# Attention, mixture of experts and feed-forward on one core: another order of the feed-forward's second products, and x loaded in two halves

## The chip, the core and the metric

The kernel runs on one NeuronCore of a Trainium2 chip. The metric is the device time of one execution in microseconds (us). TensorE multiplies into PSUM, VectorE (DVE), ScalarE (ACT) and GpSimd (POOL) do the rest of the arithmetic, and SyncE (SP) issues nearly all DMAs. Each engine works through its own instructions in the order in which they are written.

## The reference, cut to what matters

```python
attn = softmax(mask(q k^T / 8 + bias)) @ v        # 4 x 8 heads, 576 x 64, window 128
x = attn as (2304, 512)
P = exp(x @ w_gate - max); 8 rounds of row and column scaling
out = sum over e of P[:, e] * (relu(x @ w1[e]) @ w2[e])   # 8 experts, 512 -> 1024 -> 512
h = out @ w_in                                    # 512 -> 2048
g = where(h >= 1, h, where(h <= -1, 0, (h + 1)**2 / 4))
return g @ w_out                                  # 2048 -> 512
```

The change concerns the last three lines, the feed-forward, and the loads of x into SBUF.

## The kernel before, in words

Every fp32 operand is split into a high part h (rounded, by ScalarE, line 705 in the feed-forward) and a low part l (the rest, by VectorE, line 708), and one product is three matmuls: high by high (L76), high by low (L77), low by high (L78). This is `mm3`, and one call of it is called a step here.

The feed-forward is cut into three thirds of 768 tokens; a third has eight units of 256 columns of h, taken in pairs. Both its matrix products are done with seven block products in place of eight. For a pair, `g1` runs twice (the first product of unit one, then of unit two, 42 matmuls of 384 columns each, PSUM banks a to d), and then `g2s` once, the second product for both units: 42 steps of three matmuls of 256 columns. It has 21 results (3 blocks n of 128 tokens by 7 block products s); two results share a PSUM bank of tag "g2", of which there are four (bufs=4). So there are eleven fills of a bank, the last with one result. A result needs one step of unit one and one of unit two. When a bank's results are complete, `drain` adds it to `acf` in SBUF (VectorE, L841; in the first pair of a third ScalarE copies it, L839). The fifth fill can start when the first bank is drained.

Before the change, `g2s` begins with unit one's step for the first half of four banks, and then goes bank by bank: unit two's step for the first half, both units' steps for the second half, drain, and unit one's step for the first half of the bank after the next three.

Between the two products stands `put7`, a generator. It makes from the first product of a unit the seven blocks of g and their high and low parts: `choose` (L702) is the piecewise function, whose square ScalarE makes before (L698, L699); blocks 0, 1, 2 are c22, f11, c12; blocks 3, 4 are s13 and 5, 6 are s24, two sums each, made by GpSimd (L726, L727, L731, L732). `hi(n, m)` and `lo(n, m)` make the parts of blocks n to m-1. A unit's `put7` starts in its own `g1` and goes one part further at each tick. A tick comes after each block product of `g1` and after each third step of `g2s`; this sets where its instructions stand on VectorE, ScalarE and GpSimd, between the drains. In a pair, unit one's last part `lo(5, 7)` falls into the last tick before `g2s`, and unit two's `put7` is half done when `g2s` starts. s13 and s24 lie in two buffers of tag "raw", which the next unit's s13 and s24 take over.

`xload` loads the next third's x, high and low, four DMAs each, one every four ticks. In the feed-forward it starts at a third's last `g2s`; the loads then fall into that `g2s` and the first products after it. There too SyncE loads w2 for the first pair of a third, twice over (`w2_prep` is appended by both the previous pair and the first), and writes the third's results to `out` (`combine`, L798).

```python
NPUT = 4
def tick(first): ...      # advances every put7 by one part, then weight loads, x loads, sums
run(g1(i + 1, pools, ps2), True)
run(g2s(i, acc, ps2), False)
```

Of the kernel before, what the change touches and what calls it, by code (L numbers as in the profile page):

```python
# [11 lines left out]
F32 = mybir.dt.float32  # L12
# [17 lines left out]
def attn_moe_ffn(ctx: ExitStack, tc, q, k, v, w_gate, w1, w2, w_in, w_out, out):  # L30
    nc = tc.nc
# [43 lines left out]
    def mm3(ps, lh, ll, rh, rl, first, last, on=False):  # L75
        nc.tensor.matmul(ps, lhsT=lh, rhs=rh, start=first, stop=False, skip_group_check=on)  # L76
        nc.tensor.matmul(ps, lhsT=lh, rhs=rl, start=False, stop=False, skip_group_check=on)  # L77
        nc.tensor.matmul(ps, lhsT=ll, rhs=rh, start=False, stop=last, skip_group_check=on)  # L78
# [323 lines left out]
                    nc.sync.dma_start(out=d[:, :, a - p * TP:z - p * TP], in_=x.bitcast(F32))  # L402

    def xload(p):
        for x, d in zip(xop[p % 2], xd[p]):
            for kk in range(KD):
                nc.sync.dma_start(out=x[:, kk].bitcast(F32), in_=d[:, kk])
                for _ in range(4):
                    yield

    def logits(t0, n, lp, wgs, tag):
        nt = n // P
# [250 lines left out]
    def g1(i, pools, psp):  # L663
        kind, t, e, j = units[i]
        wh, wl = W1.pop(i)
        V, G = nc.vector, nc.gpsimd
        p = phase(i)

        def prod(ps, b, a, first):
            ah, al = (S["h"][:, a], S["l"][:, a]) if isinstance(a, int) else (xq(p, *a), xq(p, *a, True))  # L670
            for kk in range(KH):
                mm3(ps, wh[:, kk, b, :], wl[:, kk, b, :], ah[:, kk, :], al[:, kk, :],
                    first and kk == 0, kk == KH - 1, not first)

        def bank(x):
            return psp.tile([P, TH], F32, tag=x, name=f"ps{x}")

        def tmp(x):
            return tmpp.tile([P, TH], F32, tag=x, name=x)

        def put(c, f, r):

            h, l = (x[:, f, r, :] for x in ht)
            nc.scalar.activation(h, c, AF.Relu)  # L684
            yield "V"
            V.scalar_tensor_tensor(l, c, 0.0, h.bitcast(F32), ALU.max, ALU.subtract)  # L686
            yield ""

        def put7(c11, pc, pd, u2, c22):

            h, l = ht
            hf = h.bitcast(F32)
            f11, c21, c12 = (tmp(x) for x in ("f11", "c21", "c12"))
            g = tp.tile([P, 2, TH], F32, tag="T", name="g")
            s13, s24 = (rawp.tile([P, 2, TH], F32, tag="raw", name=x) for x in ("s13", "s24"))

            def square(c, n):
                nc.scalar.activation(g[:, n], c, AF.Relu, bias=half, scale=0.5)  # L698
                nc.scalar.activation(g[:, n], g[:, n], AF.Square)  # L699

            def choose(o, c, n):
                V.scalar_tensor_tensor(o, c, 1.0, g[:, n], ALU.max, ALU.min)  # L702

            def hi(n, m, x):
                nc.scalar.activation(h[:, n:m], x, AF.Copy)  # L705

            def lo(n, m, x):
                V.tensor_tensor(l[:, n:m], x, hf[:, n:m], ALU.subtract)  # L708

            square(c22, 0)  # L710
            square(c11, 1)
            yield ""
            choose(c22, c22, 0)
            V.tensor_tensor(c21, pc, u2, ALU.add)
            hi(0, 1, c22.unsqueeze(1))
            yield ""
            choose(f11, c11, 1)
            lo(0, 1, c22.unsqueeze(1))
            V.tensor_tensor(c12, pd, u2, ALU.add)
            square(c21, 0)  # L720
            hi(1, 2, f11.unsqueeze(1))
            yield ""
            choose(c21, c21, 0)
            lo(1, 2, f11.unsqueeze(1))
            square(c12, 1)
            G.tensor_tensor(s13[:, 0], c21, c22, ALU.add)  # L726
            G.tensor_tensor(s13[:, 1], f11, c21, ALU.subtract)  # L727
            yield ""
            choose(c12, c12, 1)
            hi(2, 3, c12.unsqueeze(1))  # L730
            G.tensor_tensor(s24[:, 0], s13[:, 0], f11, ALU.subtract)  # L731
            G.tensor_tensor(s24[:, 1], c12, s24[:, 0], ALU.subtract)  # L732
            yield "free"
            lo(2, 3, c12.unsqueeze(1))
            yield "free"
            hi(3, 5, s13)
            yield "free"
            lo(3, 5, s13)
            yield "free"
            hi(5, 7, s24)  # L740
            yield "free"
            lo(5, 7, s24)
            yield "free"

        pa, pb = (bank("a"), bank("b")) if i % 2 == 0 else (bank("b"), bank("a"))
        pc, pd = bank("c"), bank("d")
        p1, u2, u3 = (tmp(x) for x in ("p1", "u2", "u3"))
        prod(pa, 0, (0, 0), True)
        nc.scalar.activation(p1, pa, AF.Copy)  # L749
        yield  # L750
        hop = pools["hop"]
        if kind == 0:
            ht = HT[i] = [hop.tile([P, 2, 2, TH], F32R, tag=f"h{x}", bufs=2, name=f"h{x}") for x in "hl"]
            c12, c21, c22 = (pools["c"].tile([P, TH], F32, tag=x, bufs=2, name=x) for x in ("c12", "c21", "c22"))
        else:
            ht = HT[i] = [hop.tile([P, 7, TH], F32R, tag=f"h{x}", bufs=2, name=f"h{x}") for x in "hl"]
            c22 = tmp("c22")
        prod(pb, 4, 1, True)
        V.tensor_tensor(u2, pb, p1, ALU.add)  # L759
        yield  # L760
        prod(pc, 5, (1, 0), True)
        V.tensor_tensor(u3, pc, u2, ALU.add)  # L762
        yield
        prod(pd, 3, 0, True)
        V.tensor_tensor(c22, pd, u3, ALU.add)  # L765
        yield
        prod(pa, 1, (0, 1), False)
        if kind == 0:
            c11 = put(pa, 0, 0)
            puts.append(c11)  # L770
        else:
            puts.append(put7(pa, pc, pd, u2, c22))
        yield
        prod(pc, 6, (1, 1), False)
        if kind == 0:
            NEXT[c11] = next(c11)
            V.tensor_tensor(c21, pc, u2, ALU.add)  # L777
            puts.append(put(c22, 1, 1))
        yield
        prod(pd, 2, 2, False)  # L780
        if kind == 0:
            V.tensor_tensor(c12, pd, u2, ALU.add)
            puts.append(put(c21, 0, 1))
        yield
        if kind == 0:
            puts.append(put(c12, 1, 0))
# [21 lines left out]
    def g2s(i, acc, psp):  # L808
# [4 lines left out]
        end = i + 2 == NU  # L813
        flat = acc.rearrange("p n s d -> p (n s) d")
        if end:
            order = [(0, 0), (0, 1), (1, 0), (1, 1), (0, 2), (1, 2), (2, 0), (2, 1), (0, 3), (0, 4), (1, 3), (1, 4),
                     (0, 5), (0, 6), (1, 5), (1, 6), (2, 3), (2, 5), (2, 2), (2, 4), (2, 6)]
        else:
            order = [(n, s) for s in range(7) for n in range(NB)]
        banks = [sorted(order[x:x + 2]) for x in range(0, len(order), 2)]  # L820
# [3 lines left out]
        def part(b, x, u):  # L824
            if x == 0 and u == 0:
                PS[b] = psp.tile([P, 2, FU], F32, tag="g2", bufs=4, name="psg2")
            n, s = banks[b][x]
            hh, hl, wh, wl = ops[u]
            ts = slice(n * P, (n + 1) * P)
            mm3(PS[b][:, x], hh[:, s, ts], hl[:, s, ts], wh[:, BLOCK[s]], wl[:, BLOCK[s]], u == 0, u == 1)  # L830
            count[0] += 1
            return count[0] % 3 == 0

        def drain(b):
            f = [n * 7 + s for n, s in banks[b]]
            a = flat[:, f[0]:f[-1] + 1:max(f[-1] - f[0], 1)]
            ps = PS.pop(b)[:, 0:len(f)]
            if first:
                nc.scalar.activation(a, ps, AF.Copy)  # L839
            else:  # L840
                nc.vector.tensor_tensor(a, ps, a, ALU.add)  # L841
# [8 lines left out]
            r0 = t * TP + r * TH + (NB - 1) * P  # L850
            nc.sync.dma_start(out=out[r0:r0 + P, x * FU:(x + 1) * FU], in_=n2[s])

        for b in range(4):
            if part(b, 0, 0):
                yield
        for b in range(len(banks)):
            if b >= 4 and part(b, 0, 0):
                yield
            for x, u in [(0, 1), (1, 0), (1, 1)][:1 if len(banks[b]) == 1 else 3]:
                if part(b, x, u):  # L860
                    yield
            drain(b)
            if end:
                if b in (6, 7):
                    post.append(combine(t, [b - 6], acc, (V, G)))
                elif b == 8:
                    add(V, 5, 1)
                    add(V, 3, 5)
                    add(G, 6, 3)
                elif b == 9:  # L870
                    add(G, 0, 4)
                    add(G, 0, 5)
                    store(0, 1, 0)
                elif b == 10:
                    store(6, 0, 1)
                    add(V, 3, 4)
                    store(3, 1, 1)
                    add(V, 2, 1)
                    store(2, 0, 0)
# [374 lines left out]
```

## Time and profile before

| | |
|---|---|
| median of three runs | 2112.09 us (2112.01 to 2113.35) |
| profiled execution | 2110.97 us, its span 2109.2 us |
| TensorE busy | 2042.0 us (97%), 11719 matmuls |
| VectorE / ScalarE / GpSimd busy | 1336.0 / 746.1 / 728.3 us |
| mean granted TensorE clock | 0.995 |

The span is from the first to the last instruction; the feed-forward takes the part from about 1686 us to the end. TensorE is busy for nearly all of it, but matmuls overlap, so a gap of TensorE shorter than a matmul's latency is not seen as idle: the start times of the matmuls tell more than the idle times.

### The profile page before, as it was taken

How to read it: one execution, taken by the hardware profiler on the slowest of the kernel's cores; microseconds unless marked ns; L12 is line 12 of the kernel's file. 1: busy time of each engine (PE TensorE's matmuls, PEld its weight loads, DVE VectorE, ACT ScalarE, POOL GpSimd, SP SyncE). 2: the span in 40 equal slices, each digit the busy share in tenths (PEclk: the TensorE clock that was granted, in tenths of full speed). 3: DMA queues.
4: the chain of work that ended last, by engine and by line, in shares of the span. 5: the costliest groups of instructions: out<-in, count | busy, mean ns of one | idle time of the engine just before them, and what ended most of it. 6: DMA issues, size and time to landing. Idle time of an engine off the chain costs nothing.

```text
span 2109.2 us, 32062 instructions
## 1 busy us (share of the span) xinstructions
PE 2042.0 (97%) x11719; PEld 1854.7 (88%) x11719; DVE 1336.0 (63%) x2967; ACT 746.1 (35%) x1716; POOL 728.3 (35%) x755
## 2 busy tenths in 40 slices
PE   7999999999999999999999999999999999899997
PEld 5888888998999898998899898999899898898887
DVE  6766655554554756666666666666666667857686
ACT  6777343333333331221121231121121263545452
POOL 4333347666756401112121011111110036645433
PEclk9999999999999999999999999999999999999999
DMA  7333578777777787676677597676676684866762
GB/s 154 86 82 95 205 244 308 244 261 249 255 254 248 270 328 252 245 245 239 234 257 242 208 338 266 234 262 223 233 276 214 215 327 177 315 256 261 281 238 100
DMA packets 238797, 496.91 MB, mean 236 GB/s; under 512 B 70704, under 2 KB 152624, under 8 KB 238640
## 3 DMA queue, kind: packets, MB, share of 16 engines
q1 hardware_dynamic: 222640, 475.34, 63.8%
q10 hardware_dynamic: 16000, 19.53, 3.0%
q8 instruction: 92, 1.51, 0.3%
q14 instruction: 65, 0.53, 0.1%
HBM read 353.39 MB, written 141.03 MB: 234 GB/s over the span
## 4 chain that ended last, share of the span: by engine, by line
PE 82%; DVE 7%; ACT 6%; DMA 3%; issue 1%; SPq 1%; POOL 0%; ACTq 0%; POOLq 0%; DVEq 0%
PE psg L78 15%; PE psg L76 14%; PE psg L77 14%; PE psc L76 3%; PE psc L77 3%; PE psc L78 3%; PE psd L76 3%; PE psd L77 3%; PE psd L78 3%; PE psb L76 2%; PE psb L78 2%; PE psb L77 2%; PE psa L77 2%; PE psa L78 2%; PE psa L76 2%; ACT g L698 2%
## 5 line engine op out<-in xcount | busy, mean ns | idle before, releaser
L78 PE MATMUL psg<-w2h,hl 128*128 128x512 f32 (+1 forms) x1584 | 568.6, 359 | 22.1 <-DVE hl L708 21.5
L76 PE MATMUL psg<-w2h,hh 128*128 128x512 f32 (+1 forms) x1584 | 567.1, 358 | 7.7 <-DVE acc L907 2.7
L77 PE MATMUL psg<-w2l,hh 128*128 128x512 f32 (+1 forms) x1584 | 564.4, 356 | 6.1 <-DMA w2l<-wd2l 6.1
L78 PEld LDWEIGHTS psg<-w2h,hl 128*128 128x128 f32 x1584 | 300.1, 189 | 72.9 <-DVE hl L708 30.5
L907 DVE SCALAR_TENSOR_TENSOR acc<-psg,pt,acc 128x512 f32<-128x512 f32 x252 | 188.2, 749 | 252.1 <-PE psg L78 250.7
L76 PEld LDWEIGHTS psg<-w2h,hh 128*128 128x128 f32 x1584 | 300.3, 190 | 52.1 <-ACT hh L705 8.2
L77 PEld LDWEIGHTS psg<-w2l,hh 128*128 128x128 f32 x1584 | 300.3, 190 | 47.3 <-DMA w2l<-wd2l 7.3
L684 ACT ACTIVATE hh<-c 128x384 fp32r<-128x384 f32 x270 | 140.8, 521 | 87.4 <-DVE c L777 53.8
L686 DVE SCALAR_TENSOR_TENSOR hl<-c,hh 128x384 fp32r<-128x384 f32 x270 | 165.0, 644 | 0.0
L749 ACT ACTIVATE p<-psa 128x384 f32<-128x384 f32 x57 | 28.0, 492 | 368.5 <-PE psa L78 338.6
L76 PE MATMUL psd<-sh,w1h 128*128 128x384 f32 x456 | 153.9, 338 | 1.6 <-DVE c L765 1.6
L78 PE MATMUL psd<-sh,w1l 128*128 128x384 f32 x456 | 153.3, 336 | 0.0
L77 PE MATMUL psd<-sl,w1h 128*128 128x384 f32 x456 | 153.2, 336 | 0.0
L192 POOL TENSOR_TENSOR t<-e 128x128 f32<-128x128 f32 x32 | 15.1, 471 | 372.9 <-DVE e L168 372.9
L193 POOL TENSOR_TENSOR t<-e,t 128x128 f32<-128x128 f32 x32 | 15.5, 484 | 326.7 <-DVE e L168 326.7
L726 POOL TENSOR_TENSOR s<-c,c 128x384 f32<-128x384 f32 x24 | 30.2, 1259 | 283.6 <-DVE c L702 283.6
L82 POOL TENSOR_TENSOR w2l<-raw,w2h 128x512 fp32r<-128x512 f32 x60 | 81.5, 1381 | 117.9 <-ACT w2h L81 117.9
L343 POOL TENSOR_TENSOR s<-s,mx 128x512 f32<-128x512 f32 (+2 forms) x80 | 66.6, 848 | 124.9 <-DVE mx L341 71.5
L759 DVE TENSOR_TENSOR u<-psb,p 128x384 f32<-128x384 f32 x57 | 31.8, 557 | 103.2 <-PE psb L78 79.8
L76 PE MATMUL psc<-x0h,w1h 128*128 128x384 f32 x272 | 92.7, 341 | 1.6 <-DVE u L762 1.6
L78 PE MATMUL psc<-x0h,w1l 128*128 128x384 f32 x272 | 92.4, 340 | 0.0
L77 PE MATMUL psc<-x0l,w1h 128*128 128x384 f32 x272 | 92.3, 339 | 0.0
(273 smaller groups left out, 4725.3 us busy)
## 6 DMA issues: line engine op xcount, KB each, us to landing
w1h<-wd1h SPq DMA_DIRECT2D x84, 896.0 KB, 5.0
w1l<-wd1l SPq DMA_DIRECT2D x84, 896.0 KB, 7.8
raw<-in_moe_w SPq DMA_DIRECT2D x60, 512.0 KB, 4.5
w2h<-wd2h SPq DMA_DIRECT2D x60, 512.0 KB, 5.6
w2l<-wd2l SPq DMA_DIRECT2D x60, 512.0 KB, 6.4
wd1h<-w1h SPq DMA_DIRECT2D x30, 896.0 KB, 6.2
wd1l<-w1l SPq DMA_DIRECT2D x30, 896.0 KB, 6.5
w2h<-wd2h SPq DMA_DIRECT2D x28, 896.0 KB, 8.1
```

Source lines behind the costliest of these rows:

```text
L76: nc.tensor.matmul(ps, lhsT=lh, rhs=rh, start=first, stop=False, skip_group_check=on)
L77: nc.tensor.matmul(ps, lhsT=lh, rhs=rl, start=False, stop=False, skip_group_check=on)
L78: nc.tensor.matmul(ps, lhsT=ll, rhs=rh, start=False, stop=last, skip_group_check=on)
L82: eng.tensor_tensor(l, x, h.bitcast(F32), ALU.subtract)
L343: nc.gpsimd.tensor_tensor(s[:, 0:nj, :nk], s[:, 0:nj, :nk], mx[:, 6:6 + nj].unsqueeze(2).to_broadcast([P, nj, nk]), ALU.mult)
L684: nc.scalar.activation(h, c, AF.Relu)
L686: V.scalar_tensor_tensor(l, c, 0.0, h.bitcast(F32), ALU.max, ALU.subtract)
L698: nc.scalar.activation(g[:, n], c, AF.Relu, bias=half, scale=0.5)
L726: G.tensor_tensor(s13[:, 0], c21, c22, ALU.add)
L749: nc.scalar.activation(p1, pa, AF.Copy)
L759: V.tensor_tensor(u2, pb, p1, ALU.add)
L907: nc.vector.scalar_tensor_tensor(a, ps, sc, a, ALU.mult, ALU.add)
```

## The change

Three edits. In `g2s`, unit one's steps for both halves of four banks come first; then, bank by bank, unit two's two steps, the drain, and, from the second bank on, unit one's two steps for the bank that stands three further on. Only a bank's first step has the start flag, since both halves are now begun before either is complete. For the last pair of all, the results of token block 2 move behind those of blocks 0 and 1. In `put7`, unit one's `hi(5, 7)` and `lo(5, 7)` come three ticks later. In `xload`, the four high parts come three ticks apart, then there is a pause of 20 ticks, and then the four low parts follow, three ticks apart.

```diff
     def xload(p):
-        for x, d in zip(xop[p % 2], xd[p]):
-            for kk in range(KD):
-                nc.sync.dma_start(out=x[:, kk].bitcast(F32), in_=d[:, kk])
-                for _ in range(4):
-                    yield
+        for n in range(2 * KD):
+            lo, kk = divmod(n, KD)
+            nc.sync.dma_start(out=xop[p % 2][lo][:, kk].bitcast(F32), in_=xd[p][lo][:, kk])
+            for _ in range(20 if n == KD - 1 else 3):
+                yield
@@ put7
             lo(3, 5, s13)
             yield "free"
+            for _ in range(3 if i % 2 == 0 else 0):
+                yield "free"
             hi(5, 7, s24)
             yield "free"
             lo(5, 7, s24)
@@ g2s
-            mm3(PS[b][:, x], hh[:, s, ts], hl[:, s, ts], wh[:, BLOCK[s]], wl[:, BLOCK[s]], u == 0, u == 1)
+            mm3(PS[b][:, x], hh[:, s, ts], hl[:, s, ts], wh[:, BLOCK[s]], wl[:, BLOCK[s]], u == 0 and x == 0, u == 1,
+                True)
...
-        for b in range(4):
-            if part(b, 0, 0):
-                yield
-        for b in range(len(banks)):
-            if b >= 4 and part(b, 0, 0):
-                yield
-            for x, u in [(0, 1), (1, 0), (1, 1)][:1 if len(banks[b]) == 1 else 3]:
+        def bank(b, u):
+            for x in range(len(banks[b])):
                 if part(b, x, u):
                     yield
+
+        for b in range(4):
+            yield from bank(b, 0)
+        for b in range(len(banks)):
+            yield from bank(b, 1)
             drain(b)
+            if 1 <= b < len(banks) - 3:
+                yield from bank(b + 3, 0)
             if end:
-                if b in (6, 7):
-                    post.append(combine(t, [b - 6], acc, (V, G)))
+                if b in (5, 6):
+                    post.append(combine(t, [b - 5], acc, (V, G)))
```

What this does to the order of the instructions is shown at three places; they stand in each pair alike (the first two) or once in each of two thirds (the third).

TensorE, the second pair of the first third, where the fifth fill of a bank begins. Unit one's operands are w2h_17434 and hh_17438, unit two's w2h_17448 and hh_17523; psg2 with its number is a fill. Before, the 16th step (of the fourth fill, 17615) and the 17th, which begins the fifth fill (17678):

```order
L76 MATMUL psg2_17615<-w2h_17448,hh_17523 128x256
L77 MATMUL psg2_17615<-w2l_17449,hh_17523 128x256
L78 MATMUL psg2_17615<-w2h_17448,hl_17524 128x256
L76 MATMUL psg2_17678<-w2h_17434,hh_17438 128x256
L77 MATMUL psg2_17678<-w2l_17435,hh_17438 128x256
L78 MATMUL psg2_17678<-w2h_17434,hl_17439 128x256
```

In the changed kernel, the 12th step (of the second fill, 17598) and the 13th, which begins the fifth fill (17662):

```order
L76 MATMUL psg2_17598<-w2h_17448,hh_17523 128x256
L77 MATMUL psg2_17598<-w2l_17449,hh_17523 128x256
L78 MATMUL psg2_17598<-w2h_17448,hl_17524 128x256
L76 MATMUL psg2_17662<-w2h_17434,hh_17438 128x256
L77 MATMUL psg2_17662<-w2l_17435,hh_17438 128x256
L78 MATMUL psg2_17662<-w2h_17434,hl_17439 128x256
```

The fifth fill, which takes the first fill's bank, begins after 12 steps instead of 16, and one bank, two steps, after the first fill's last step instead of three banks and nine steps after it.

VectorE, the same pair, from unit two's first `choose` to the second row after `lo` of c12. hl_17439 is unit one's low part, hl_17524 unit two's; acf is a drain. Before:

```order
L702 SCALAR_TENSOR_TENSOR c22_17525<-c22_17525,g_17563 128x384
L714 TENSOR_TENSOR c21_17561<-psc_17505,u2_17508 128x384
L708 TENSOR_TENSOR hl_17439<-s24_17477,hh_17438 128x768
L702 SCALAR_TENSOR_TENSOR f11_17560<-psb_17503,g_17563 128x384
L708 TENSOR_TENSOR hl_17524<-c22_17525,hh_17523 128x384
L719 TENSOR_TENSOR c12_17562<-psd_17506,u2_17508 128x384
L702 SCALAR_TENSOR_TENSOR c21_17561<-c21_17561,g_17563 128x384
L708 TENSOR_TENSOR hl_17524<-f11_17560,hh_17523 128x384
L702 SCALAR_TENSOR_TENSOR c12_17562<-c12_17562,g_17563 128x384
L841 TENSOR_TENSOR acf_17084<-psg2_17593,acf_17084 128x2x256
L708 TENSOR_TENSOR hl_17524<-c12_17562,hh_17523 128x384
L841 TENSOR_TENSOR acf_17084<-psg2_17597,acf_17084 128x2x256
```

In the changed kernel:

```order
L702 SCALAR_TENSOR_TENSOR c22_17525<-c22_17525,g_17563 128x384
L714 TENSOR_TENSOR c21_17561<-psc_17505,u2_17508 128x384
L702 SCALAR_TENSOR_TENSOR f11_17560<-psb_17503,g_17563 128x384
L708 TENSOR_TENSOR hl_17524<-c22_17525,hh_17523 128x384
L719 TENSOR_TENSOR c12_17562<-psd_17506,u2_17508 128x384
L702 SCALAR_TENSOR_TENSOR c21_17561<-c21_17561,g_17563 128x384
L708 TENSOR_TENSOR hl_17524<-f11_17560,hh_17523 128x384
L702 SCALAR_TENSOR_TENSOR c12_17562<-c12_17562,g_17563 128x384
L708 TENSOR_TENSOR hl_17439<-s24_17477,hh_17438 128x768
L708 TENSOR_TENSOR hl_17524<-c12_17562,hh_17523 128x384
L844 TENSOR_TENSOR acf_17085<-psg2_17591,acf_17085 128x2x256
L844 TENSOR_TENSOR acf_17085<-psg2_17598,acf_17085 128x2x256
```

Unit one's `lo(5, 7)` (hl_17439 from s24_17477) moves from ahead of f11 to behind `choose` of c12, and the first drain moves from ahead of unit two's `lo` of c12 to behind both.

SyncE, the loads around the first pair of the second third: w2 twice, x1l, out, then w1. Before:

```order
L620 DMA w2h_18527<-wd2h_1_0_0_8553 128x1792
L620 DMA w2l_18528<-wd2l_1_0_0_8554 128x1792
L407 DMA x1l_4177<-xd5l_76 128x768
L620 DMA w2h_18540<-wd2h_1_0_1_8557 128x1792
L620 DMA w2l_18541<-wd2l_1_0_1_8558 128x1792
L798 DMA out<-acf_17084 128x3x256 x4
L407 DMA x1l_4177<-xd5l_76 128x768 x2
L620 DMA w1h_18699<-wd1h_1_0_2_8559 128x1792
L620 DMA w1l_18700<-wd1l_1_0_2_8560 128x1792
L407 DMA x1l_4177<-xd5l_76 128x768
L620 DMA w1h_18718<-wd1h_1_0_3_8563 128x1792
L620 DMA w1l_18719<-wd1l_1_0_3_8564 128x1792
```

In the changed kernel:

```order
L620 DMA w2h_18527<-wd2h_1_0_0_8553 128x1792
L620 DMA w2l_18528<-wd2l_1_0_0_8554 128x1792
L620 DMA w2h_18539<-wd2h_1_0_1_8557 128x1792
L620 DMA w2l_18540<-wd2l_1_0_1_8558 128x1792
L800 DMA out<-acf_17085 128x3x256 x4
L620 DMA w1h_18693<-wd1h_1_0_2_8559 128x1792
L620 DMA w1l_18694<-wd1l_1_0_2_8560 128x1792
L620 DMA w1h_18712<-wd1h_1_0_3_8563 128x1792
L620 DMA w1l_18713<-wd1l_1_0_3_8564 128x1792
L407 DMA x1l_4177<-xd5l_76 128x768 x4
```

The four loads of x1l stand behind the loads of w2 and w1 and the stores, instead of among them.

## Rows read from the trace of the kernel before

**Rows 1.** Waits of TensorE, 1700 to 2100 us: engine, line, releaser, total us, times, longest.
```profile
PE psg L78 <- DVE hl L708: 21.5, 31, 1.1
PE psg L77 <- DMA w2l<-wd2l: 6.1, 4, 2.7
```

**Rows 2.** Five stretches: us, TensorE busy (instructions), granted clock, DMA share, GB/s.
```profile
1702.08:1720.88 18.80, 16.64 (x127) 1.00 0.75 304
1769.17:1788.04 18.87, 16.38 (x127) 1.00 0.26 100
1836.78:1860.95 24.17, 18.59 (x128) 0.79 0.90 349
1976.85:1997.19 20.34, 16.55 (x127) 1.00 0.87 334
2079.36:2098.21 18.85, 16.65 (x127) 1.00 0.00 1
```

**Rows 3.** TensorE in time, pair of 1769.17: start, us, line, tiles, idle before.
```profile
1772.44 0.38 PE L78 MATMUL psg<-w2h,hl 128*128 128x256 f32 x1 [1.01 <-DVE hl L708]
...
1779.19 0.39 PE L78 MATMUL psg<-w2h,hl 128*128 128x256 f32 x1 [1.08 <-DVE hl L708]
...
1787.92 0.28 PE L78 MATMUL psg<-w2h,hl 128*128 128x256 f32 x1
```

**Rows 4.** VectorE in time, same pair.
```profile
1770.49 0.96 DVE L708 TENSOR_TENSOR hl<-s,hh 128x768 fp32r<-128x768 f32 x1
...
1773.23 0.56 DVE L708 TENSOR_TENSOR hl<-f,hh 128x384 fp32r<-128x384 f32 x1
1774.09 0.98 DVE L702 SCALAR_TENSOR_TENSOR c<-c,g 128x384 f32<-128x384 f32 x1 [0.30 <-ACT g L699]
1774.99 0.68 DVE L841 TENSOR_TENSOR acf<-psg,acf 128x512 f32<-128x512 f32 x1
1775.66 0.70 DVE L708 TENSOR_TENSOR hl<-c,hh 128x384 fp32r<-128x384 f32 x1
...
1777.48 1.66 DVE L708 TENSOR_TENSOR hl<-s,hh 128x768 fp32r<-128x768 f32 x1
```

**Rows 5.** ScalarE in time, same pair.
```profile
1773.53 0.53 ACT L699 ACTIVATE g<-g 128x384 f32<-128x384 f32 x1
1775.10 0.53 ACT L705 ACTIVATE hh<-c 128x384 fp32r<-128x384 f32 x1 [1.04 <-DVE c L702]
```

**Rows 6.** GpSimd in time, same pair.
```profile
1773.39 1.26 POOL L726 TENSOR_TENSOR s<-c,c 128x384 f32<-128x384 f32 x1 [3.87 <-DVE c L702]
1774.61 1.34 POOL L727 TENSOR_TENSOR s<-f,c 128x384 f32<-128x384 f32 x1
```

**Rows 7.** Two stretches at the lower clock, columns as in the second group.
```profile
1844.75:1850.47 5.72, 5.72 (x27) 0.50 1.06 409
...
41.52:44.92 3.40, 3.34 (x18) 0.50 0.09 20
```

**Rows 8.** TensorE in time, pair of 1836.78.
```profile
1838.20 0.39 PE L77 MATMUL psg<-w2l,hh 128*128 128x256 f32 x1 [1.15 <-DMA w2l<-wd2l]
...
1841.49 0.55 PE L76 MATMUL psg<-w2h,hh 128*128 128x256 f32 x1 [1.73 <-DMA w2h<-wd2h]
1844.75 0.58 PE L77 MATMUL psg<-w2l,hh 128*128 128x256 f32 x1 [2.71 <-DMA w2l<-wd2l]
```

**Rows 9.** TensorE in time, pair of 1976.85.
```profile
1979.41 0.36 PE L76 MATMUL psg<-w2h,hh 128*128 128x256 f32 x1 [0.70 <-DMA w2h<-wd2h]
1981.74 0.39 PE L77 MATMUL psg<-w2l,hh 128*128 128x256 f32 x1 [1.97 <-DMA w2l<-wd2l]
```

**Rows 10.** ScalarE in time, pair of 1976.85.
```profile
1985.47 1.09 ACT L839 ACTIVATE acf<-psg 128x512 f32<-128x512 f32 x2 [1.62 <-DMA out<-acf]
```

**Rows 11.** DMA issues of SyncE before and in the pair of 1836.78.
```profile
1828.82 0.42 SPq L407 DMA_DIRECT2D x1l<-xd5l  x1
...
1840.71 3.40 SPq L407 DMA_DIRECT2D x1l<-xd5l  x2
```

More of the change, by code (lines that the diff above doesn't have):

```diff
@@ L815, in g2s @@
         if end:
-            order = [(0, 0), (0, 1), (1, 0), (1, 1), (0, 2), (1, 2), (2, 0), (2, 1), (0, 3), (0, 4), (1, 3), (1, 4),
-                     (0, 5), (0, 6), (1, 5), (1, 6), (2, 3), (2, 5), (2, 2), (2, 4), (2, 6)]
+            order = [(0, 0), (0, 1), (1, 0), (1, 1), (0, 2), (1, 2), (0, 3), (0, 4), (1, 3), (1, 4), (0, 5), (0, 6),
+                     (1, 5), (1, 6), (2, 0), (2, 1), (2, 3), (2, 5), (2, 2), (2, 4), (2, 6)]
         else:
```

## The prediction

> **What bounds the kernel now.** I read the engine table first: TensorE is busy 97% of the span, with no other engine above 63%. So only what delays TensorE, or changes its clock, moves the time. The waits of TensorE over the feed-forward's first two thirds come second. One line recurs: the third matmul of a step, L78, waits for a low part that VectorE makes (L708), 21.5 us in 31 waits; four waits for the loads of w2l cost 6.1 [rows 1]. No wait for a drain stands among the large ones. Third, the windows of single second products say what a pair costs. An ordinary one takes 18.87 us, the first of the first third 18.80, the very last 18.85; the first pair of the second third takes 24.17 at a mean clock of 0.79, that of the last third 20.34 [rows 2]. Fourth, the timeline of one ordinary pair. From 1779.19 to 1787.92 lie 72 steps of one matmul start to the next [rows 3]: 0.12 us each, so 0.36 for a step of three matmuls and 15.1 for the 126 of a second product. So an ordinary pair loses 18.87 - 15.1 = 3.7 us, and the two waits of 1.01 and 1.08 [rows 3] with the slow restart behind each and some short gaps are that loss. All ends of the change must be found in these 12 windows and in what x's loads disturb.
>
> **The ordinary pair, nine of the twelve.** I count from its start, T = 1769.17. In the new order the fifth fill begins after 12 steps, at T + 4.3, if the steps before it have their parts. It takes over the first fill's bank, so it needs that fill's drain, and only the second fill's two steps lie between (the two fences on TensorE in the section on the change). Before, nine steps did. The wait added is therefore TensorE on VectorE's first drain; queued behind it are all 30 steps left.
>
> When does that drain come? By VectorE's new row, after `choose` of c12, unit one's moved `lo(5, 7)` and `lo` of c12. Before, `choose` of c12 began at T + 4.92, when ScalarE's square was there [rows 4, 5]. `lo(5, 7)`, 0.96 us, is gone from ahead of f11 [rows 4], which is ahead of all that chain, so `choose` now begins at T + 3.96. It then costs 0.98, as it did beside GpSimd's sums of 1.26 and 1.34 [rows 4, 6]. The moved `lo(5, 7)` has 768 columns; such a one took 0.96 in one place and 1.66 in another [rows 4]. GpSimd is at the sums of s13 and s24 just then, so I take 1.66. `lo` of c12 takes 0.55 (0.56 for f11's [rows 4]), the drain 0.68. Neighbours on VectorE start 0.08 before the end of the one ahead (1774.99 against 1774.09 + 0.98 [rows 4]), three times. So 3.96 + 0.98 + 1.66 + 0.55 + 0.68 - 0.24 = 7.6, and TensorE goes on at T + 7.7: one standstill of 3.4 us. From there 30 steps of 0.36 are 10.8, and 0.1 of restart makes 18.6. Unit two's later parts are then no longer waited for: its second pair of low parts was there at 1779.19, T + 10.0 [rows 3], and the new order first needs them nine steps after the standstill, T + 10.9. So the waits of before are not added to the new one; they are replaced by it. 18.6 against 18.85: -0.25 a pair, nine times -2.3.
>
> The bounds: with `choose` at 0.55, as f11's is near to, and `lo(5, 7)` at 0.96 (both as if GpSimd were idle [rows 4]), the drain ends at T + 6.5, the standstill is 2.2 and the pair 17.4. At the other end `lo` of c12 costs 0.70, as before [rows 4], and the pair is 18.75. I take the upper values, since GpSimd's sums were beside the same instructions before.
>
> A rule bears on this. The rows of before show no wait of TensorE on a drain [rows 1]. The Trainium skill, Perfetto Trace Analysis, section Optimizing Tensor Performance, says that independent groups of matmuls should rotate through PSUM banks so that one's evacuation lies beside the next group's matmuls. By those rows alone the drains stay hidden (the fourth case below); by the rule the new order, with one bank between a fill's end and its bank's next use, uncovers them, which is the sum here.
>
> **The clock, the largest term.** In the pair of 1836.78 TensorE waited 1.15, then 1.73, then 2.71 us for w2 [rows 8], and after that a stretch of 5.72 us ran at 0.50, the lower of its two levels, 1.2 against 2.4 GHz [rows 7]. In the pair of 1976.85 it waited 0.70 and then 1.97 [rows 9] and the whole window kept 1.00 [rows 2]; so did the ordinary pairs with their 1.01 and 1.08. So 1.97 alone was borne, and 1.73 with 2.71 was not. One of 3.4 is longer than each: I expect a fall. Its price: 27 matmuls in 5.72 us are 0.21 each against 0.12, so 43% of the time at half speed is lost. The long stretch lost 2.5, a shorter one at 0.50, of 3.40 us [rows 7], 1.5. The low end, nothing, is what a held clock gives; a fall that lasts into the next product could cost more than 2.5. I take 1.6, near the shorter stretch, since TensorE gets work without a break after the standstill, where the long one had a second wait of 2.71 ahead of it. Nine times 1.6 is +14.4.
>
> **The first pairs of the thirds.** There ScalarE drains the first banks. In the first third its drain follows `hi` of c12 (0.53 [rows 5], behind `choose` at T + 4.94) and takes 0.55 (1.09 for two [rows 10]): TensorE goes on at T + 6.05, after 1.75, which 1.97 says the clock bears. Another wait of some 0.7 comes later, since unit two's low parts are not earlier. 6.05 + 10.8 + 0.7 = 17.6 against 18.80: -1.2.
>
> In the other two thirds the drain writes acf, which the stores of the previous results must have left. In the last third they let ScalarE go at 1985.47, T + 8.62 [rows 10], far behind the T + 5.4 at which it would be ready; the first drain ends at T + 9.2, TensorE goes on at 9.3, and the pair takes 9.3 + 10.8 + 0.1 = 20.2. The stand of 5.0 costs clock, 1.9 here, between 1.5 and 2.5: 22.1. Before, the stores ended unnoticed, since the fifth fill began four steps later, after waits for w2.
>
> In the second third x1l's loads at 1828.82 and 1840.71 (two, 3.40 [rows 11]) shared the queue with w2, of which TensorE was waiting for the last piece at 1844.75 [rows 8]. They now stand behind w2, the stores and w1 (the fence on SyncE). The w2 waits shrink to about those of the last third, where x was not being loaded, and the stores' wait takes over: 22.1 too. So 24.17 becomes 22.1, -2.1; 20.34 becomes 22.1, +1.8.
>
> **The rest at nothing.** The loads of x themselves have the rest of a third's products to hide in; none of the rows shows TensorE waiting on x. If moving them to later ticks uncovers one, I allow 1 us. The last product's blocks 0 to 2 are reordered only behind its last drain: within 1 us either way. SyncE issues as many DMAs as before.
>
> **Sum.** -2.3 + 14.4 - 1.2 - 2.1 + 1.8 = +10.6, made against the profiled execution, 2110.97 (2109.2 of span and 1.8 around it), which lies 1.1 under the median of 2112.09. That gives 2121.6 by the one and 2122.7 by the other; I say 2122.
>
> **The rivals.** A measurement of this kernel tells 0.2%, 4.2 us, from no change.
>
> *The clock holds* (the other side). Place: behind the standstill at T + 4.3 in nine pairs and behind the stores in two. If one stand with full work around it is borne, the terms left are -2.3, -1.2, 20.2 - 24.17 = -4.0 and 20.2 - 20.34 = -0.1: -7.6, so 2104.5. For it: 1.97 was borne [rows 9]. Against it: 3.4 is 1.7 times that, and 5.72 us at half speed followed 2.71 [rows 7, 8]. It decides from the count: with two first pairs at 1.9 each, -3.8 remains, and two or three ordinary pairs that fall at 1.6 bring the kernel back to no change.
>
> *VectorE frees the bank at the low end,* T + 6.5. Nine pairs at 17.4 give -13.0; the standstill of 2.2 is just above the 1.97 that was borne, so about half fall, +7; the first pairs give -1.5 together. -7.5: 2104.6. For it: 0.96 and 0.55 are what the same instructions took elsewhere in the pair [rows 4]. Against it: GpSimd's sums fall into the same time [rows 6].
>
> *The drains stay hidden,* as the waits of before have it [rows 1]: then a pair loses only its old waits in part, 16.8, nine times -2.0, with -2 in the first third's first and -2 in the second third's: some -22, 2090. Against it: the order on both engines, two steps or 0.7 us for a drain with 0.68 of its own and two parts in the queue ahead of it.
>
> *The change only trades the loads:* the wait on the drain comes to just the old 3.7 with a clock that falls in some pairs, and all that stays is -2 from x1l: 2109 to 2113. It lies between the first case and the second.
>
> **How the numbers follow.** My sum 0.62, range of its own 2113 to 2131 (falls at 1.0 to 2.5 each); clock holds 0.16; low end 0.13; hidden 0.04; traded 0.05. Faster by over 0.2% is below 2107.9: most of the second to fourth cases, 0.30. Within 0.2%, the traded one and edges of the low end: 0.10. Slower, the sum: 0.60. The range leaves out the hidden drains and the worst falls: 2100 to 2131.
>
> **What would show it.** A new wait of TensorE, L76 on VectorE's acf drain, near 3 us in each of nine pairs, and stretches at 0.50 just behind it; the 21.5 us of L78 on L708 gone or nearly; in the first pairs of the later thirds ScalarE's drain waiting on the stores and TensorE on ScalarE. Wrong would be the clock at 1.00 throughout the ordinary pairs with that wait there (first rival), the wait near 2 (second), or no such wait (third). If pairs of before and after are alike except that of 1836.78, the fourth holds.

## The result, and the profile after

The changed kernel takes 2124.69 us (median of five, 2120.87 to 2128.1) against 2112.09: a ratio of 1.0061, with a 95% interval of 1.0043 to 1.008. It is slower, by 12.6 us. The predicted time was 2122. The profiled execution has a span of 2122.6 us, 13.4 more than that of the profiled execution before.

The waits of TensorE over the feed-forward (engine, tile and line, releaser: total us, times, longest) are not those of before [rows 1]:

```profile
PE psg L76 <- DVE acf L844: 28.2, 9, 3.2
PE psg L76 <- ACT acf L842: 7.0, 4, 2.6
PE psa L76 <- DVE f L702: 1.0, 2, 0.5
PE psg L77 <- DMA w2l<-wd2l: 0.2, 1, 0.2
```

The 31 waits for low parts are gone. In their place stand nine for VectorE's drain, of 3.1 us on average, one in each ordinary pair, and four on ScalarE's drain in the first pairs of the thirds. Here are second products of the changed kernel (us, TensorE busy and instructions, granted clock, DMA share, GB/s), the first pair of each third and four ordinary pairs; they answer to [rows 2]:

```profile
1708.70:1726.17 17.47, 15.61 (x127) 1.00 0.79 314
1740.88:1761.01 20.13, 16.96 (x127) 0.92 0.29 99
1775.72:1796.82 21.10, 17.93 (x127) 0.84 0.27 94
...
1848.00:1866.42 18.42, 15.70 (x127) 1.00 1.04 398
...
1916.00:1934.49 18.49, 15.37 (x127) 1.00 0.31 107
...
1985.51:2005.33 19.82, 17.09 (x127) 0.91 0.82 310
...
2089.45:2111.05 21.60, 18.45 (x127) 0.84 0.00 1
```

Eight of the nine ordinary pairs now have a mean clock of 0.84 to 0.92; the one at 1916.00 kept 1.00 and took 18.49. Inside the second pair three stretches, same columns, show why:

```profile
1779.92:1783.37 3.45, 0.28 (x4) 0.86 0.55 223
1783.37:1789.27 5.90, 5.90 (x27) 0.50 0.00 0
1789.27:1796.82 7.55, 7.55 (x65) 1.00 0.10 15
```

TensorE stands for 3.45 us, then works for 5.9 at half speed, then at full speed to the end. VectorE in the same pair (start, us, line, tiles, idle before), with the row of TensorE that it lets go:

```profile
1779.68 0.90 DVE L702 SCALAR_TENSOR_TENSOR c<-c,g 128x384 f32<-128x384 f32 x1 [0.39 <-ACT g L699]
1780.50 1.75 DVE L708 TENSOR_TENSOR hl<-s,hh 128x768 fp32r<-128x768 f32 x1
1782.17 0.55 DVE L708 TENSOR_TENSOR hl<-c,hh 128x384 fp32r<-128x384 f32 x1
1782.64 0.68 DVE L844 TENSOR_TENSOR acf<-psg,acf 128x512 f32<-128x512 f32 x1
```

```profile
1783.37 0.58 PE L76 MATMUL psg<-w2h,hh 128*128 128x256 f32 x1 [3.17 <-DVE acf L844]
```

Counted from the pair's start, T = 1775.72, `choose` of c12 starts at T + 3.96 and the fifth fill at T + 7.65. The difference of the two profiled executions, 13.4 us, lies here (the last column is what was predicted):

| stretch | before | after | difference | predicted |
|---|---|---|---|---|
| nine ordinary second products | 170.38 | 181.23 | +10.85 | +12.1 |
| first pair, first third | 18.80 | 17.47 | -1.33 | -1.2 |
| first pair, second third | 24.17 | 18.42 | -5.75 | -2.1 |
| first pair, last third | 20.34 | 19.82 | -0.52 | +1.8 |
| the first products ahead of the last two | 30.27 | 32.86 | +2.59 | 0 |
| a stretch of the mixture's last pass | 32.99 | 37.72 | +4.73 | 0 |
| attention, up to the mixture's first product | 276.16 | 279.09 | +2.93 | untouched |

Attention is the same in both kernels; in the profiled executions of the experiments below that point came at 274.6 to 278.3 us, whatever the edit, so I take the +2.93 for the scatter of one execution.

### The profile page after: what moved, and what is told of

It reads as the page before. It is cut to its first block, busy times and chain, and to the rows that moved or that the text cites. A ratio compares the mean times of both kernels' runs of the same rounds, so it can differ in the third digit from the quotient of the medians.

```text
span 2122.6 us, 32070 instructions
## 1 busy us (share of the span) xinstructions
PE 2051.3 (97%) x11719; PEld 1869.4 (88%) x11719; DVE 1342.4 (63%) x2967; ACT 746.0 (35%) x1716; POOL 727.2 (34%) x755
## 4 chain that ended last, share of the span: by engine, by line
PE 82%; DVE 6%; ACT 5%; DMA 4%; issue 1%; SPq 1%; POOL 0%; DVEq 0%; ACTq 0%; POOLq 0%
PE psg L76 15%; PE psg L78 14%; PE psg L77 14%; PE psc L76 3%; PE psd L76 3%; PE psc L77 3%; PE psc L78 3%; PE psd L77 3%; PE psd L78 3%; PE psb L76 2%; PE psb L78 2%; PE psb L77 2%; PE psa L77 2%; PE psa L78 2%; PE psa L76 2%; PE pso L375 2%
## 5 line engine op out<-in xcount | busy, mean ns | idle before, releaser
L76 PE MATMUL psg<-w2h,hh 128*128 128x512 f32 (+1 forms) x1584 | 574.5, 363 | 38.5 <-DVE acf L844 28.2
L77 PE MATMUL psg<-w2l,hh 128*128 128x512 f32 (+1 forms) x1584 | 570.9, 360 | 0.2 <-DMA w2l<-wd2l 0.2
L76 PEld LDWEIGHTS psg<-w2h,hh 128*128 128x128 f32 x1584 | 307.3, 194 | 82.5 <-DVE acf L844 30.4
L78 PEld LDWEIGHTS psg<-w2h,hl 128*128 128x128 f32 x1584 | 306.9, 194 | 42.9 <-DVE hl L708 0.5
L77 PEld LDWEIGHTS psg<-w2l,hh 128*128 128x128 f32 x1584 | 307.5, 194 | 40.4 <-DMA w2l<-wd2l 0.4
L193 POOL TENSOR_TENSOR t<-e,t 128x128 f32<-128x128 f32 x32 | 15.5, 484 | 324.2 <-DVE e L168 324.2
```

## The experiments

Each ratio is to the kernel before on the same chip, with its 95% interval.

**One part of the change at a time.** *x_only* is the kernel before with the new `xload`; *order_only* is the changed kernel with the old one:

```diff
-        for n in range(2 * KD):
-            ...
-            for _ in range(20 if n == KD - 1 else 3):
-                yield
+        for x, d in zip(xop[p % 2], xd[p]):
+            for kk in range(KD):
+                nc.sync.dma_start(out=x[:, kk].bitcast(F32), in_=d[:, kk])
+                for _ in range(4):
+                    yield
```

> The kernel before with the new loads of x alone. Theory (the loss of the change sits in nine standstills on the first drain and the clock behind them; the loads help one pair and hurt elsewhere): ordinary second products stay at 18.9 us, the first pair of the second third falls from 24.2 to about 20, the mixture of experts' last pass gets some 4.7 us longer at its first products; in sum 2110 to 2114. Rival (the loads of x carry the loss): 2118 or more.

> The changed kernel with the old loads of x. Theory: ordinary second products 20.1 us each as in the changed kernel, nine times +1.3 = +11, first pair of the first third 17.5 (-1.3), first pair of the second third again 22 to 24 since x's low parts stand among w2: 2118 to 2123, and no long stretch lost in the mixture of experts. Rival (the loads of x carry the loss): 2110 to 2114.

x_only took 2112.72 us (1.0004, 0.9994 to 1.0014), order_only 2123.05 (1.005, 1.0036 to 1.0064). The loss is in the order. In x_only the ordinary pairs keep 18.9 us; in order_only they take 20.0 to 21.6, and none keeps the clock. The first pair of the second third, in x_only and then in order_only:

```profile
1840.94:1864.52 23.58, 18.23 (x128) 0.86 0.93 354
```

```profile
1842.62:1863.77 21.15, 17.12 (x127) 0.92 0.94 348
```

So the loads alone bring that pair 0.6 us, not the 4 that I expected of x_only; the order alone brings 3.0, and both 5.75, so that beside the new order the loads are worth another 2.7. The first products ahead of the last two thirds' first pairs are 15.16 and 15.13 in x_only and 16.45 and 16.43 in order_only: that loss belongs to the order. The stretch of the mixture's last pass, in x_only and in order_only:

```profile
1247.80:1284.30 36.50, 33.09 (x157) 0.95 0.77 281
```

```profile
1248.20:1281.10 32.90, 31.40 (x157) 1.00 0.71 265
```

With the old loads it took 32.6 to 33.0 us in four executions, with the new ones 34.5 to 38.2 in eight: this loss belongs to the loads. The medians are less sharp: x_only is 1.1 us slower than before, with an interval that reaches from a gain of 1.3 to a loss of 3.0. In the changed kernel that stretch has a mean clock of 0.95, as in x_only, and the chain there is a wait of VectorE for the load of a weight and one of TensorE for VectorE (the first row has 7.2 instead of 8.9 before; the second 1.6 instead of 3.2):

```profile
DVE e L158 <- DMA d<-in_moe_w_out: 8.9, 1, 8.9
```

```profile
PE psg L76 <- DVE acc L912: 3.2, 1, 3.2
```

**The clock by itself.** *zeros* leaves the wait and fills it:

```diff
+            if b == 1 and not first:
+                for _ in range(27):
+                    nc.tensor.matmul(PS[3][:, 0], lhsT=zeros, rhs=ops[0][0][:, 0, 0:FU], start=False, stop=False,
+                                     skip_group_check=True)
```

> The changed kernel with 27 matmuls of a block of zeros (256 columns, added to the fourth bank, the sum unchanged) put into the standstill ahead of the fifth fill in the nine ordinary pairs, some 3.2 us of work. Theory (the clock falls because TensorE stands): the drain comes when it came, the granted clock stays at 1.00, ordinary pairs 18.5 instead of 20.1, nine times -1.65 = -15: 2108 to 2112. Rival (what follows the drain is slow for another cause, such as the reading of w2 or PSUM): no change, 2122 to 2127.

It took 2108.6 us (0.9983, 0.9974 to 0.9992). TensorE's zeros and VectorE's drain in the pair of 1731.92:

```profile
1736.24 3.40 PE L869 MATMUL psg<-hh,zeros 128*128 128x256 f32 x27
```

```profile
1738.89 1.28 DVE L845 TENSOR_TENSOR acf<-psg,acf 128x512 f32<-128x512 f32 x2
```

Two of its ordinary pairs, and the first pair of the second third, which has no such filling:

```profile
1731.92:1750.51 18.59, 18.59 (x154) 1.00 0.31 108
1765.22:1783.82 18.60, 18.60 (x154) 1.00 0.31 106
...
1833.53:1853.43 19.90, 17.29 (x127) 0.91 1.01 388
```

The first drain, 0.68 of those 1.28 us, ended at T + 7.65 as in the changed kernel, and with work that changes no sum the clock held in all nine: 18.5 to 19.0 us instead of the changed kernel's 18.5 to 21.6. Standing still is what costs the clock, if not every time, and that is the difference between slower and slightly faster than before.

**Both ends of the standstill.** *bank_alone* puts two more steps ahead of it, *put7_undone* takes unit one's last parts off VectorE's queue in it (`3 if` becomes `0 if` in `put7`):

```diff
-            if 1 <= b < len(banks) - 3:
+            if end and 1 <= b < len(banks) - 3:
                 yield from bank(b + 3, 0)
+            if not end and 2 <= b < len(banks) - 2:
+                yield from bank(b + 2, 0)
```

> The changed kernel with one edit: unit two's part of the third bank comes ahead of the fifth fill (14 steps instead of 12 ahead of it, not in the last pair). Theory (the end of the standstill is set by VectorE's queue, its start by the order of the steps): TensorE still goes on at T + 7.65, but has two steps less behind it: 7.65 + 28 x 0.36 + 0.1 = 17.8 with the clock held, the standstill 2.6 instead of 3.4, a fall in some pairs (1.6 each): pairs of 17.8 to 19.4, 2106 to 2118. Rival (two steps more or less do not matter, the wait grows elsewhere): pairs of 20, 2122 to 2127.

> The changed kernel with unit one's last parts back in the last tick ahead of the second product. Theory: 0.96 us comes back ahead of f11, so choose of c12 starts at T + 4.9, but 1.75 us goes from between it and the first drain: the drain ends at T + 6.9, the standstill is 2.6, pairs of 17.9 where the clock holds and 19.5 where it falls: 2106 to 2120. Rival (the drain does not wait for VectorE's queue but for TensorE's second fill or a store): TensorE goes on at T + 7.65 as before, pairs of 20.1, 2122 to 2127.

bank_alone took 2113.46 us (1.0008, 0.9996 to 1.002). The pair of 1771.94, and TensorE in it:

```profile
1771.94:1791.27 19.33, 16.86 (x127) 0.91 0.25 96
```

```profile
1779.60 0.39 PE L76 MATMUL psg<-w2h,hh 128*128 128x256 f32 x1 [2.47 <-DVE acf L844]
```

The fifth fill starts at T + 7.66, and eight ordinary pairs take 19.3 (the last of all keeps the changed kernel's order). The wait, 2.41 to 2.49 in the eight and 2.93 in the last, still cost the clock in all nine (0.91 or 0.92). The start of the fill and the gain of the two steps came out as worked out; that the clock would hold in some pairs did not. put7_undone took 2127.58 (1.0077, 1.0061 to 1.0094), which my theory missed. Its VectorE and TensorE in the pair of 1776.30:

```profile
1781.20 0.98 DVE L702 SCALAR_TENSOR_TENSOR c<-c,g 128x384 f32<-128x384 f32 x1 [0.30 <-ACT g L699]
1782.77 0.68 DVE L708 TENSOR_TENSOR hl<-c,hh 128x384 fp32r<-128x384 f32 x1 [0.59 <-ACT hh L705]
1783.37 1.27 DVE L844 TENSOR_TENSOR acf<-psg,acf 128x512 f32<-128x512 f32 x2
```

```profile
1784.10 0.58 PE L76 MATMUL psg<-w2h,hh 128*128 128x256 f32 x1 [2.41 <-DVE acf L844]
```

That is T + 7.80, not 6.9: the 1.75 goes from ahead of the drain, but `choose` starts 0.94 later, and `lo` of c12 now waits 0.59 for ScalarE's `hi`, which had been hidden behind the 1.75. The rival's time of T + 7.65 was nearer, but not its reason: the drain starts straight behind `lo` of c12, so it does wait for VectorE's queue. Taking a piece off a queue gives only what the next input allows.

**The drain first.** *drain_first* keeps the steps and changes VectorE's row only: unit one's last part two ticks later, unit two's `lo` of c12 one.

```diff
             yield "free"
+            if i % 2:
+                yield "free"
             lo(2, 3, c12.unsqueeze(1))
...
-            for _ in range(3 if i % 2 == 0 else 0):
+            for _ in range(5 if i % 2 == 0 else 0):
```

> The changed kernel with unit one's last low part two ticks later and unit two's low part of c12 one tick later, so that VectorE's first drain comes straight behind choose of c12, ahead of both. Theory: TensorE goes on at T + 5.5 instead of T + 7.65, a standstill of 1.2 that the clock bears, then two short waits of about 0.5 each (third drain, unit two's second low parts): pairs of 16.7 to 17.2, nine times -3.2 = -29: 2092 to 2099. Rival (the wait only moves to the low parts that are now later): pairs of 18.5 to 19, 2108 to 2115.

It took 2106.78 us (0.9978, 0.9969 to 0.9986), not 2092 to 2099. TensorE in the pair of 1772.49:

```profile
1778.00 0.39 PE L76 MATMUL psg<-w2h,hh 128*128 128x256 f32 x1 [1.04 <-DVE acf L846]
1785.45 0.39 PE L76 MATMUL psg<-w2h,hh 128*128 128x256 f32 x1 [1.05 <-DVE acf L846]
```

TensorE goes on at T + 5.51, as expected, and all ordinary pairs keep the clock, but six of them take 18.1, not 17, and the last ones of the thirds 18.9 to 19.8: a second wait of 1.05 stands at T + 13, for the fifth drain behind unit two's last low part, which I had not seen coming.

*last_part_late* moves that low part three ticks on, and *last_part_late_old_x* also keeps the old loads of x up to the feed-forward's first third:

```diff
+            for _ in range(3 * (i % 2 and i + 1 < NU)):
+                yield "free"
             lo(5, 7, s24)
...
-            for _ in range(20 if n == KD - 1 else 3):
+            for _ in range(4 if p <= NPH else 20 if n == KD - 1 else 3):
```

> drain_first with unit two's last low part three ticks later (not in the last pair), so that it no longer stands ahead of VectorE's fifth to seventh drain. In drain_first each ordinary pair had two waits of 1.04 us, the second near T + 13 for the fifth drain behind that low part. Theory: the second wait goes, each wait costs 1.4 to 1.5 with its restart, pairs of 18.1 become 16.7, those of 19.8 about 18.3: some -12 in all, 2093 to 2098. Rival (the wait moves to the low part itself, needed late in the product): pairs of 17.8 to 18.1, 2104 to 2107.

> The same, but x is loaded in the old way up to the feed-forward's first third and in two halves only for the other two. Theory (the new loads cost 2 to 5 us in the mixture of experts' last pass, where they fall among its loads of a and w1): 3 us less than last_part_late, 2089 to 2095. Rival (what x costs there is scatter): equal within 1 us.

2107.42 us (0.9983, 0.9971 to 0.9995) and 2102.34 (0.9956, 0.9943 to 0.9969). The rival won the first: the second wait moved to the low part itself, a wait of 0.69 to 0.9 on L708 in the ordinary pairs and 2.4 in two of them, pairs of 17.8 to 18 and of 20.4. (In the last pair of all, here and below, unit one's last part keeps its old place.) The old loads gave 5 us by the medians; in the profiles that stretch of the mixture took 32.6 instead of 35.1, which is half of it.

*one_bank_more* joins what helped: the three-bank order of bank_alone, drains first, unit two's first double part ahead of unit one's last (`7 if`), unit two's last two ticks late, the loads of the kernel just above.

> The same loads as the one before; three banks instead of two get unit two's part before the fifth fill begins (14 steps, not in the last pair), unit two's first double low part stands ahead of unit one's last, and unit two's last comes two ticks late. Theory (what counts is how many steps lie between a fill's end and its bank's next use): the first wait of 1.04 shrinks to 0.3 or goes, no other comes: pairs of 15.5 to 16.2, 2082 to 2090. Rival (low parts of blocks 3 and 4 are needed at step 22 and come at T + 8.5 to 9): a wait of about 1 there instead, pairs of 16.7, 2090 to 2096.

It took 2099.64 us (0.9947, 0.9934 to 0.9961), the fastest here and faster than both kernels. One of its ordinary pairs:

```profile
1765.62:1782.92 17.30, 16.14 (x127) 1.00 0.29 107
```

Six ordinary pairs take 17.2 to 17.3 in place of 18.9, with a wait of 0.3 on the drain; the last pairs of the thirds take 19.1 to 19.6. I had expected 15.5 to 16.2, or 16.7: two short waits come later, 0.26 for ScalarE's high part and 0.49 for the low part, each with its restart. In its very last pair two short waits, 1.9 us apart, were followed by a fall of the clock:

```profile
2065.65:2085.26 19.61, 17.77 (x127) 0.91 0.00 1
```

```profile
2070.31 0.39 PE L78 MATMUL psg<-w2h,hl 128*128 128x256 f32 x1 [0.79 <-DVE hl L708]
2072.20 0.38 PE L76 MATMUL psg<-w2h,hh 128*128 128x256 f32 x1 [0.79 <-DVE acf L848]
```

**The sums behind a third.** *late_sums* starts them six ticks later in the changed kernel, to see whether they delay the first products of 16.4 us.

```diff
+        for _ in range(6 if len(ns) == NB else 0):
+            yield
```

> The changed kernel with the sums behind the first and the second third begun six ticks later, past the first product's first u2, u3 and c22 on VectorE. Theory: the two first products of 16.4 us lose their wait, 14.7 to 15.2, since the sums no longer stand ahead of unit one's parts; but the stores go out some 6 us later, ScalarE's first drain waits for them until T + 13 or so, and the first pairs of those thirds take 22 to 26 instead of 18.4 and 19.8: 2126 to 2136 in all. Rival (the stores' wait is not what ends ScalarE's wait, w2 is): the pairs stay at 18.4 to 20, 2120 to 2123.

2136.92 us (1.0113, 1.0097 to 1.013), just above the range of 2126 to 2136, and for another reason. The first products took 17.4, not 14.7 to 15.2. The first pairs took 23.5 and 23.8, but not for the stores, for which ScalarE no longer waited at all; TensorE waited for unit two's parts:

```profile
PE psg L78 <- DVE hl L708: 5.4, 4, 2.4
```

In both kernels TensorE waits in these first products for rows that stand behind the sums on VectorE (0.51 in the changed kernel, 1.28 and 0.79 here). What exactly makes the 16.4 stays open: in the changed kernel three drains stand at the very end of the product, and the first sum takes 2.50 beside GpSimd's sums where it took 1.30 before, but no run took these alone away. In bank_alone, where one drain less falls to the very end, they took 15.7.

```profile
1830.70 1.74 DVE L844 TENSOR_TENSOR acf<-psg,acf 128x512 f32<-128x512 f32 x3 [0.39 <-PE psg L78]
1832.36 2.50 DVE L805 TENSOR_TENSOR acf<-acf 128x768 f32<-128x768 f32 x1
```

## Why the prediction was right, and where it was not

**The new wait** was the step on which all rested, and it came as worked out: T + 7.65 against T + 7.7, with `choose` of c12 at 0.90 (0.98 taken), the moved part at 1.75 (1.66), `lo` at 0.55, the drain at 0.68. The upper bounds were the right ones, and waits on L708 vanished. (By the new order unit two's second low parts are first needed ten steps after the standstill, not nine, which leaves them a little more time.) drain_first confirms the place: with only VectorE's row changed, the end of the wait moved to T + 5.51. The Trainium skill (Perfetto Trace Analysis, Optimizing Tensor Performance) asks that independent groups rotate through PSUM banks, so that the evacuation of one overlaps the next group's matmuls. The trace agrees: with only one bank left for that overlap, TensorE waited 28.2 us for drains.

**The clock** was predicted at 1.6 a pair. The pair that kept it took 18.49 (18.6 predicted), and the nine average 20.14: 1.65. Behind that average stand eight falls of 1.85 and one pair without, so a slightly low price and a fall too many cancelled. zeros shows the cause.

**The first pair of the first third** came out too, 17.47 against 17.6, with a wait of 1.41 where 1.75 was put. The second wait, 0.45 where 0.7 was put, was one for ScalarE's drain at T + 10.9 and not for unit two's low parts: there the size was luck.

**The first pairs of the later thirds** are the step that failed: 22.1 each was predicted, 18.42 and 19.82 came. I let the stores free ScalarE at T + 8.6 and TensorE at 9.3; it went on at T + 7.5. In the last third ScalarE's row answers to [rows 10], with a wait of 0.86 instead of 1.62:

```profile
1992.31 0.60 ACT L842 ACTIVATE acf<-psg 128x512 f32<-128x512 f32 x1 [0.86 <-DMA out<-acf]
```

That is T + 6.8, mostly since T itself came 1.3 us later, behind the longer first product. And the clock charge of 1.9 was due only once: after waits of 2.63 and 2.56 the one pair kept 1.00, the other fell to 0.91. I also put the gain of the second third down to the loads of x; x_only gives them 0.6 by themselves, and 3.0 came with the order alone.

**Loads and first products at nothing** was wrong the other way: +2.6 for the first products, and about 3.5 in the mixture's last pass (the means of the eight and four executions, 36.3 and 32.8), where I had allowed 1. There "the rest of a third's products" did not hide the loads: VectorE waited longer for a weight, 8.9 instead of 7.2. How the loads of x delay that weight no run takes apart.

So 2122 was right in its largest terms, and that the rest nearly cancelled is luck: by the table, the first pairs came out 6.1 us better than predicted and the ordinary ones 1.3, the first products and the mixture 7.3 worse, and scatter added 2.9.

## What to carry to other kernels

When accumulation steps are moved ahead to fill a wait, count the steps that are left between a bank's last matmul and its next first one, and walk the draining engine's queue over just that gap: here two steps of 0.36 us stood against a queue of 3 us. The wait by itself cost no more than those that it replaced (18.49 us in the pair that kept the clock, against 18.9 before); the clock behind it made the loss. The drain first in its queue turned the loss of 0.6% into a gain of 0.2% (drain_first); with one bank more in between, the low parts moved again and the old loads of x in the mixture it was 0.5%.

So a wait of TensorE can have a second price, the clock behind it. In drain_first two waits of 1.04 and 1.05, 7.5 us apart, were borne, where one of 3.17 mostly was not. Short waits are no guarantee, though: in the last pair of one_bank_more the clock fell behind two of 0.79.

## What the runs showed of the hardware

Matmuls on zeros were worth their place: 27 of them in each of nine standstills made the kernel some 16 us faster than the same kernel without them, by the two medians, since the granted clock stayed at 1.00. The length of a standstill alone did not tell whether the clock would fall: waits of 2.41 to 2.93 us dropped it in all nine ordinary pairs of bank_alone, while waits of 2.63 and 3.12 in the changed kernel (1848.00 and 1916.00) did not. Two waits of about 0.8, 1.9 us apart, were followed by a fall in the last pair of last_part_late, last_part_late_old_x and one_bank_more; no other ordinary pair of these runs had one.
